# Sigmoid attention and a SiLU MLP on one core: a quad's heads regrouped so that one DMA loads all 128 partitions

## The chip, the cores and the metric

The kernel runs on one core of a Trainium2 chip. The metric is the device time of one execution in microseconds; before the change it is 379.75 us, the median of three runs (379.59 to 379.92).

The engines are named as in the profile. PE multiplies matrices, and PEld is its load of the stationary operand ("weights"); DVE and ACT work elementwise and move results out of PSUM; POOL here only makes an identity matrix and issues DMAs; SP issues DMAs. Transfers themselves run on 16 DMA engines that all queues share.

## The reference

Cut to what matters, in float32:

```python
q, k, v: (8, 12, 448, 64)          # batch, heads, sequence, head_dim
w_in: (768, 2048); w_out: (2048, 768)

scores = q @ k.T / sqrt(64) - log(448)
attn = sigmoid(scores) @ v                       # per batch and head
x = attn.transpose(0, 2, 1, 3).reshape(8 * 448, 12 * 64)
h = x @ w_in
out = (h * sigmoid(h)) @ w_out                   # (3584, 768)
```

A column of `x`, and so a row of `w_in`, belongs to one head and one of its 64 dimensions.

## The kernel before

**Quads and units.** Attention works in 24 quads: a batch and four of its 12 heads (`g = 3 * b + iq`). A quad's q, k or v lies in one tile `[128, 2, 7, 64]` in fp16 (`qf`, `kf`, `vf`; `new_flat`, line 66): the lower 64 partitions hold two heads (`j` = 0, 1), the upper 64 two others. A partition holds 7 neighbouring rows of the sequence, so the 448 rows are 64 partitions by 7 chunks. Before the change the lower half has heads `2 * iq` and `2 * iq + 1`, the upper half heads `6 + 2 * iq` and `7 + 2 * iq`; `load` (line 71) therefore issues two DMAs per tile, each over 64 partitions, from POOL, which converts float32 to fp16 on the way (112 KB written for each half).

A unit is one quad and one of its 7 chunks of keys (168 units). `scores` (line 177) makes 4 matmuls of a unit into PSUM (`psc`, two buffers), and ACT turns them into `attnT` with one sigmoid (line 202). `values` (line 213) multiplies them with `vf` in 7 rounds of 4 matmuls (`pav`), one round per unit, and DVE moves the two sums of a quad into `xT[b]`, whose 6 column blocks are pairs of heads. q and k must be transposed first: for quads 0 to 5 on PE through an identity matrix (`pe_transpose`, line 140), for the others by a DMA (`dma_transpose`, line 159) after DVE or ACT has put the rows in order.

**The MLP.** `h_unit` (line 250) makes one of 16 blocks of h per batch, 6 matmuls on `xT` and `w_in_sb`, with a sigmoid on ACT and a product on DVE. `out_set` multiplies with `w_out`. `w_in_sb` holds the 768 rows of `w_in` as 6 blocks of 128 partitions, one for each pair of heads; `load_w_in` (line 106) loads a quarter of the 2048 columns, which four h units use, with one DMA.

**What sets the order.** Every engine runs its instructions in the order in which the kernel writes them down. POOL's queue is: the first two chunks of k of quad 0, the identity, the rest of that k, then k and q of quad 1, v of 0, k and q of 2, v of 1 and 2, k and q of 3, and the first quarter of w_in (lines 455 to 464); later loads are written down behind transposes and values (`after_transpose`, `after_values`). POOL's DMAs take eight semaphores in turn, so that an issue waits for the landing of the eighth DMA before it. The first q does not go through POOL: SP and ACT load it as float32 into a spare tile (`load_first_q`, line 89), and DVE (chunks 0 to 3) and ACT (chunks 4 to 6) convert it (lines 469 and 470). Before it is there, PE runs nine dummy matmuls.

The first 24 units are followed by a table written by hand, `behind` (line 542), which says what PE does after the scores of each unit: dummy matmuls (`keep_busy`), transposes, some rounds of `values` (`rounds`), and, as the first work on w_in, four of the six matmuls of h units 0 and 1 (`begin`). After unit 23 the order comes from `stretch` (line 435), which deals out MLP matmuls between bursts of scores by a budget of nanoseconds.

Of the kernel before, what the change touches and what calls it, by code (L numbers as in the profile page):

```python
# [17 lines left out]
def kernel(  # L18
# [9 lines left out]
    nc = tc.nc  # L28

    B, H, S, D = q.shape  # L30
    NT, DMODEL = out.shape
    DFF = moe_w_in.shape[1]
    P = 128
    HP = P // 2
    NCH = S // HP
    NPAIR = H // 2
    NQ = NPAIR // 2
# [22 lines left out]

    source = {"q": q, "k": k, "v": v}
    flat = {}

    def new_flat(name, g):
        flat[name, g] = (p3 if name == "v" else p4).tile(
            [P, 2, NCH, D], F16, tag=f"{name}f", name=f"{name}f"
        )

    def load(names, g, c0=0, c1=NCH):
        b, iq = divmod(g, NQ)
        for name in names:
            if (name, g) not in flat:
                new_flat(name, g)
            for half in range(2):
                h0 = half * (H // 2) + 2 * iq
                nc.gpsimd.dma_start(  # L78
                    flat[name, g][half * HP : (half + 1) * HP, :, c0:c1].rearrange(
                        "p i c d -> p i (c d)"  # L80
                    ),
                    source[name][b, h0 : h0 + 2].rearrange("i (p c) d -> p i (c d)", c=NCH)[
                        :, :, c0 * D : c1 * D
                    ],
                )

    FIRST, SPLIT = 2, 4

    def load_first_q():
        room = cpool.tile([P, NHC * NO2 // 2], F32, tag="T2", name="qs")  # L90
        st = room[:, : 2 * NCH * D].rearrange("p (i c d) -> p i c d", i=2, c=NCH)
        for half, eng in ((0, nc.sync), (1, nc.scalar)):
            h0 = half * (H // 2)
            eng.dma_start(
                st[half * HP : (half + 1) * HP].rearrange("p i c d -> p i (c d)"),
                q[0, h0 : h0 + 2].rearrange("i (p c) d -> p i (c d)", c=NCH),
            )
        return st

    ident = cpool.tile([P, P], F16, tag="ident", name="ident")  # L100
    bias_s = cpool.tile([P, 1], F32, tag="biass", name="bias_s")
# [1 line left out]
    w_in_sb = cpool.tile([P, NCC, DFF], F16, tag="w_in_sb", name="w_in_sb")  # L103
    w_out_sb = cpool.tile([P, NFC, DMODEL], F16, tag="w_out_sb", name="w_out_sb")

    def load_w_in(step):
        cols = slice(step * DFF // 4, (step + 1) * DFF // 4)
        nc.gpsimd.dma_start(
            w_in_sb[:, :, cols], moe_w_in[:, cols].rearrange("(cc p) f -> p cc f", p=P)
        )  # L110

    def load_w_out(nh, part):
        cols = slice(nh * NO2, (nh + 1) * NO2)
# [23 lines left out]
    def act_copy(o, i):  # L137
        nc.scalar.activation(o, i, AF.Copy)
# [286 lines left out]
    def rows_if_any():  # L425
        if later:
            g, name = later.pop(0)
            dma_transpose(g, name, nc.vector.tensor_copy)
            if name == "q" and g + 4 < NQB and g + 4 > 12:
                load("kq", g + 4)  # L430
# [4 lines left out]
    def stretch(ns):  # L435
# [14 lines left out]
                middle = math.inf  # L450
        late_sigmoid()

    first_q = load_first_q()
    new_flat("q", 0)
    load("k", 0, 0, FIRST)
    make_identity(nc, ident)
    load("k", 0, FIRST, NCH)
    load("kq", 1)
    load("v", 0)
    load("kq", 2)  # L460
    load("v", 1)
    load("v", 2)
    load("kq", 3)
    load_w_in(0)

    nc.vector.memset(dummy, 0.5)
    nc.vector.memset(bias_s, NEG_LOG_S)
    nc.scalar.activation(warm, bias_s, AF.Sigmoid, bias=bias_s, scale=1.0)
    nc.vector.tensor_copy(flat["q", 0][:, :, :SPLIT], first_q[:, :, :SPLIT])
    act_copy(flat["q", 0][:, :, SPLIT:], first_q[:, :, SPLIT:])  # L470

    units = [(g, ch) for g in range(NQB) for ch in range(NCH)]
    waiting = []
# [3 lines left out]
    def after_transpose(g):  # L477
        if g == 0:
            load("kq", 4)
            load_w_in(1)  # L480
        elif g == 1:
            load("kq", 5)
        elif g == 4:
            load("kq", 8)

    def after_values(g):
        if g == 0:
            load("v", 3)
            load_w_in(2)
            load_w_in(3)  # L490
        elif g == 1:
            load("v", 4)
            load_w_out(0, 0)
            load_w_out(0, 1)
        elif g == 2:
            load("v", 5)
            load_w_out(1, 0)
            load_w_out(1, 1)
            load("kq", 6)
            load("kq", 7)  # L500
        elif g + 3 < NQB:
            load("v", g + 3)
        if g == 6:
            for to in (10, 11, 12):
                load("kq", to)
        if g == 5:
            load("kq", 9)
        if g >= 6 and g + 3 < NQB:
            later.extend(((g + 3, "k"), (g + 3, "q")))
# [28 lines left out]
    def begin(fc, steps):  # L538
# [20 lines left out]
        17: ((rounds, 1, 7),),  # L559
        18: ((rounds, 2, 2),),  # L560
        19: ((rounds, 2, 4),),
        20: ((begin, 0, 4),),
        21: ((rounds, 2, 6),),
        22: ((rounds, 2, 7),),
        23: ((begin, 1, 4),),
    }
# [68 lines left out]
```

## Time and profile before

| | us |
|---|---|
| median of the runs | 379.75 |
| the profiled execution | 379.66 |
| its span on the core | 377.9 |
| PE busy | 368.4 (97%) |
| ACT busy | 242.7 (64%) |
| DVE busy | 234.2 (62%) |
| POOL busy, mostly issuing DMAs | 93.2 (25%) |

The chain that ended last is PE for 90% of the span. Its other shares stand in the first 26 us: DMA 3%, POOL 4%, ACT 2%. By line, PE's share is 39% in `ph` (h, line 257), 34% in `po` (output, line 333), 9% in the scores (line 191) and 7% in the values (line 227).

The granted clock of PE is full throughout. The DMA engines are busy for 80% or more of nearly every slice in the first 90 us, at up to 205 GB/s written; that counts the fp16 bytes, and twice as many float32 bytes are read for them. A busy DMA share above 1 means that packets overlap on an engine.

How to read the rows: a group's row gives the line, the engine, the operation, output and inputs by the program's names, the number of instructions, their busy time in us and the mean of one in ns, then the idle time of the engine just before them and what ended it. A row of waits gives who waited for whom: total us, times, longest. A row of the chain or of a timeline begins with its start in us and its duration.

### The profile page before, as it was taken

To read this page: it belongs to the slowest core of one execution; us is meant where nothing else is said; L and a number is where in the kernel's file an instruction comes from. 1 tells how busy PE (TensorE), PEld (TensorE's weight loads), DVE (VectorE), ACT (ScalarE), POOL (GpSimd) and SP (SyncE) were. 2 spreads that over 40 slices of the span, in tenths; PEclk is the share of its full clock that TensorE was granted. 3 is DMA by queue.
4 is the path that set the end of the run, shared out by engine and by line. 5 is a ranking of instruction groups with operands and counts; after the bars stand their busy time and mean duration, and the time that the engine had idled before them with its cause. 6 is when DMAs were issued, how large, how long until landed. Compare 5 with 4: busy or idle time off the path is not lost.

```text
span 377.9 us, 7695 instructions
## 1 busy us (share of the span) xinstructions
PE 368.4 (97%) x3081; PEld 189.1 (50%) x3081; DVE 234.2 (62%) x417; ACT 242.7 (64%) x355; POOL 93.2 (25%) x158
## 2 busy tenths in 40 slices
PE   6989999999999999999999999999999999999995
PEld 2544445555554445545555544544555455555663
DVE  2546646996666566648577557645677457556773
ACT  4998886868777776576556676667866685244000
POOL 8846325402744304303132303101011000000000
PEclk9999999999999999999999999999999999999999
DMA  8999999994999999929399856745065300110233
GB/s 126 179 189 204 205 203 166 135 146 95 170 195 140 179 111 120 149 61 112 62 166 193 94 117 93 76 111 75 0 136 97 84 2 2 50 35 0 81 87 83
DMA packets 66403, 42.80 MB, mean 113 GB/s; under 512 B 37056, under 2 KB 62912, under 8 KB 66368
## 3 DMA queue, kind: packets, MB, share of 16 engines
q0 software_dynamic: 28032, 22.59, 44.3%
q1 hardware_dynamic: 38112, 19.41, 30.5%
q8 instruction: 24, 0.39, 0.4%
q10 hardware_dynamic: 224, 0.33, 0.3%
q14 instruction: 11, 0.09, 0.1%
HBM read 45.61 MB, written 11.01 MB: 150 GB/s over the span
## 4 chain that ended last, share of the span: by engine, by line
PE 90%; POOL 4%; DMA 3%; ACT 2%; issue 1%; DVE 0%; ACTq 0%; POOLq 0%
PE ph L257 39%; PE po L333 34%; PE psc L191 9%; PE pav L227 7%; DMA w_in_sb<-in_moe_w_in_dram 3%; POOL kf L78 2%; ACT attnT L202 1%; POOL vf L78 1%; POOL qf L78 1%; PE ptrq L148 0%; PE ptrk L148 0%; ACT attnT L175 0%; DVE gTr L271 0%; DVE osb L341 0%; ACT kept L402 0%
## 5 line engine op out<-in xcount | busy, mean ns | idle before, releaser
L202 ACT ACTIVATE attnT<-psc,bias_s 128x896 f16<-128x896 f32 (+1 forms) x168 | 138.1, 900 | 46.3 <-PE psc L191 46.3
L257 PE MATMUL ph<-xT,w_in_sb 128*128 128x448 f16 x768 | 151.1, 353 | 0.8 <-DMA w_in_sb<-in_moe_w_in_dram 0.8
L271 DVE TENSOR_TENSOR gTr<-ph,tsig 128x448 f16<-128x448 f32 x128 | 78.2, 622 | 69.3 <-ACT tsig L269 68.8
L257 PEld LDWEIGHTS <-w_in_sb 128*128 128x128 f16 x768 | 72.9, 98 | 74.2 <-issue 8.0
L269 ACT ACTIVATE tsig<-ph 128x448 f16<-128x448 f32 x128 | 68.2, 548 | 49.5 <-PE ph L257 49.2
L78 POOL DMA_DIRECT2D vf<-in_v_dram x48 | 28.9, 619 | 141.1 <-PE pav L227 119.8
L333 PEld LDWEIGHTS <-S 128*128 128x128 f16 x448 | 42.3, 98 | 33.5 <-issue 7.2
L341 DVE SCALAR_TENSOR_TENSOR osb<-po,osb 128x384 f32<-128x384 f32 x70 | 37.6, 553 | 22.8 <-PE po L333 22.4
L191 PE MATMUL psc<-qT,kT 64*64 64x448 f16 x672 | 48.4, 360 | 2.3 <-ACT attnT L202 0.9
L238 DVE TENSOR_SCALAR xT<-pav 128x448 f16<-128x448 f32 x48 | 27.7, 619 | 31.5 <-PE pav L227 31.5
L333 PE MATMUL po<-T,S 128*128 128x384 f16 x224 | 40.6, 327 | 0.0
L333 PEld LDWEIGHTS <-gTr 128*128 128x128 f16 x304 | 28.7, 98 | 23.5 <-issue 5.4
L333 PE MATMUL po<-w_out_sb,S 128*128 128x384 f16 x224 | 39.9, 326 | 0.0
L227 PE MATMUL pav<-attnT,vf 64*64 64x448 f16 x672 | 38.1, 349 | 0.4 <-DVE gTr L271 0.4
L78 POOL DMA_DIRECT2D qf<-in_q_dram x46 | 27.6, 612 | 31.5 <-DMA w_out_sb<-in_moe_w_out_dram 12.6
L333 PE MATMUL po<-w_out_sb,gTr 128*128 128x384 f16 x192 | 34.9, 327 | 0.0
L78 POOL DMA_DIRECT2D kf<-in_k_dram x50 | 30.3, 618 | 10.7 <-DMA vf<-in_v_dram 4.4
L191 PEld LDWEIGHTS <-kT 64*64 64x64 f16 x672 | 16.4, 105 | 30.3 <-issue 26.1
L175 ACT ACTIVATE attnT<-psc,bias_s 128x896 f16<-128x896 f32 x26 | 26.5, 1021 | 0.0
L341 DVE SCALAR_TENSOR_TENSOR osb<-po,m 128x384 f32<-128x384 f32 x42 | 23.2, 552 | 5.3 <-PE po L333 4.2
L227 PEld LDWEIGHTS <-vf 64*64 64x64 f16 x672 | 20.5, 107 | 12.0 <-issue 1.9
L348 ACT ACTIVATE m<-po 128x384 f32<-128x384 f32 x14 | 6.9, 494 | 23.7 <-PE po L333 23.7
(42 smaller groups left out, 152.2 us busy)
## 6 DMA issues: line engine op xcount, KB each, us to landing
out_dram<-osb SPq DMA_DIRECT2D x54, 192.0 KB, 3.0
vf<-in_v_dram POOLq DMA_DIRECT2D x48, 112.0 KB, 4.6
kf<-in_k_dram POOLq DMA_DIRECT2D x46, 112.0 KB, 5.9
qf<-in_q_dram POOLq DMA_DIRECT2D x46, 112.0 KB, 6.1
w_in_sb<-in_moe_w_in_dram POOLq DMA_DIRECT2D x4, 768.0 KB, 10.7
w_out_sb<-in_moe_w_out_dram POOLq DMA_DIRECT2D x4, 768.0 KB, 17.0
kT<-kr SPq DMA_TRANSPOSE x18, 5.9
qT<-qr SPq DMA_TRANSPOSE x18, 6.7
```

Source lines behind the costliest of these rows:

```text
L78: nc.gpsimd.dma_start(flat[name, g][half * HP : (half + 1) * HP, :, c0:c1].rearrange("p i c d -> p i (c d)"), source[name][b, h0 : h0 + 2] ...
L175: nc.scalar.activation(to, psc, AF.Sigmoid, bias=bias_s, scale=QKSCALE)
L191: nc.tensor.matmul(banks[j][own, :S], qkT["k", g][rows, ch, own], qkT["q", g][rows, :, own], start=True, stop=True,)
L202: nc.scalar.activation(to, psc, AF.Sigmoid, bias=bias_s, scale=QKSCALE)
L227: nc.tensor.matmul(pav[half][j * D : (j + 1) * D, :S], flat["v", g][own, j, ch, :], at[own, j, :], start=(ch == 0), stop=(ch == NCH - 1),)
L238: nc.vector.tensor_scalar_mul(xT[b][:, half * NQ + iq, :], pav[half][:, :S], SX)
L257: nc.tensor.matmul(ph[:, :S], w_in_sb[:, cc, fc * P : (fc + 1) * P], xT[b][:, cc, :], start=(at == 0), stop=(at == NCC - 1),)
L269: nc.scalar.activation(tsig, ph[:, :S], AF.Sigmoid, bias=0.0, scale=ISX)
L271: nc.vector.tensor_mul(gTr[:, fc, (b % 2) * S : (b % 2) * S + S], ph[:, :S], tsig)
L333: nc.tensor.matmul(po[:, :NO2], a[:, fc, :], w[:, fc, :], start=(fc == 0), stop=(fc == NHC - 1))
L341: nc.vector.scalar_tensor_tensor(out=o, in0=po, scalar=sign, in1=x, op0=ALU.mult, op1=ALU.add)
L348: nc.scalar.activation(m1, po, AF.Copy, scale=ISX)
```

## The change

The grouping of heads changes. A quad is now four neighbouring heads `4 * iq` to `4 * iq + 3`, with head `4 * iq + 2 * j + h` in slot `j` of half `h`. Two neighbouring heads then fill 128 partitions at one even step through memory, so one DMA loads a whole tile (`rows_in`). Each pair of heads in `xT` is now heads that are two apart, and `w_in`'s rows must be permuted to match: a block of 128 partitions takes 64 rows of one head and 64 of another that is not its neighbour. `load_w_in` does this with four DMAs of 64 partitions and three blocks each. The first q is cut between SP and ACT by chunks and no longer by halves of the partitions, so each of the two casts reads what one DMA brought. In the table, two entries change places: rounds 4 and 5 of values(2) now stand after unit 20, and the first four matmuls on w_in after unit 21.

The number of instructions on PE, DVE and ACT stays the same; on POOL the rows of the program go from 159 to 103.

```diff
+    def rows_in(name, g):
+        b, iq = divmod(g, NQ)
+        return source[name][b, 4 * iq : 4 * iq + 4].rearrange(
+            "(i h) (p c) d -> (h p) i (c d)", h=2, c=NCH
+        )
+
     def load(names, g, c0=0, c1=NCH):
-        b, iq = divmod(g, NQ)
         for name in names:
             if (name, g) not in flat:
                 new_flat(name, g)
-            for half in range(2):
-                h0 = half * (H // 2) + 2 * iq
-                nc.gpsimd.dma_start(
-                    flat[name, g][half * HP : (half + 1) * HP, :, c0:c1].rearrange(
-                        "p i c d -> p i (c d)"
-                    ),
-                    source[name][b, h0 : h0 + 2].rearrange("i (p c) d -> p i (c d)", c=NCH)[
-                        :, :, c0 * D : c1 * D
-                    ],
-                )
+            nc.gpsimd.dma_start(
+                flat[name, g][:, :, c0:c1].rearrange("p i c d -> p i (c d)"),
+                rows_in(name, g)[:, :, c0 * D : c1 * D],
+            )
...
-        st = room[:, : 2 * NCH * D].rearrange("p (i c d) -> p i c d", i=2, c=NCH)
-        for half, eng in ((0, nc.sync), (1, nc.scalar)):
-            h0 = half * (H // 2)
+        at = 0
+        for c0, c1, eng in ((0, SPLIT, nc.sync), (SPLIT, NCH, nc.scalar)):
+            size = 2 * (c1 - c0) * D
+            st = room[:, at : at + size]
+            at += size
             eng.dma_start(
-                st[half * HP : (half + 1) * HP].rearrange("p i c d -> p i (c d)"),
-                q[0, h0 : h0 + 2].rearrange("i (p c) d -> p i (c d)", c=NCH),
+                st.rearrange("p (i e) -> p i e", i=2), rows_in("q", 0)[:, :, c0 * D : c1 * D]
             )
-        return st
+            yield flat["q", 0][:, :, c0:c1], st.rearrange("p (i c d) -> p i c d", i=2, d=D)
...
     def load_w_in(step):
         cols = slice(step * DFF // 4, (step + 1) * DFF // 4)
-        nc.gpsimd.dma_start(
-            w_in_sb[:, :, cols], moe_w_in[:, cols].rearrange("(cc p) f -> p cc f", p=P)
-        )
+        rows = moe_w_in[:, cols].rearrange("(iq j h d) f -> h j d iq f", j=2, h=2, d=D)
+        for half in range(2):
+            for j in range(2):
+                nc.gpsimd.dma_start(
+                    w_in_sb[j * D : (j + 1) * D, half * NQ : (half + 1) * NQ, cols], rows[half, j]
+                )
...
-    first_q = load_first_q()
     new_flat("q", 0)
+    casts = list(load_first_q())
...
-    nc.vector.tensor_copy(flat["q", 0][:, :, :SPLIT], first_q[:, :, :SPLIT])
-    act_copy(flat["q", 0][:, :, SPLIT:], first_q[:, :, SPLIT:])
+    nc.vector.tensor_copy(*casts[0])
+    act_copy(*casts[1])
...
-        20: ((begin, 0, 4),),
-        21: ((rounds, 2, 6),),
+        20: ((rounds, 2, 6),),
+        21: ((begin, 0, 4),),
```

## The prediction

> **What bounds the kernel now.** I read the page first, then the waits of PE, then the chain that ended last between 15 and 33 us, then ACT's timeline, and last the landing of each early DMA.
>
> ```profile
> span 377.9 us, 7695 instructions
> PE 368.4 (97%) x3081; PEld 189.1 (50%) x3081; DVE 234.2 (62%) x417; ACT 242.7 (64%) x355; POOL 93.2 (25%) x158
> L257 PE MATMUL ph<-xT,w_in_sb 128*128 128x448 f16 x768 | 151.1, 353 | 0.8 <-DMA w_in_sb<-in_moe_w_in_dram 0.8
> L78 POOL DMA_DIRECT2D qf<-in_q_dram x46 | 27.6, 612 | 31.5 <-DMA w_out_sb<-in_moe_w_out_dram 12.6
> ```
>
> PE is busy for 97% of the span; POOL, whose work the change halves, for 25%. So the change can only pay where PE is idle, or where it is busy but held to another engine's pace. The waits of PE are few:
>
> ```profile
> PE pw L135 <- DVE bias_s L467: 1.5, 1, 1.5
> PE psc L191 <- ACT attnT L202: 0.9, 2, 0.5
> PE ph L257 <- DMA w_in_sb<-in_moe_w_in_dram: 0.8, 1, 0.8
> PE psc L191 <- ACT qT L138: 0.6, 1, 0.6
> PE pav L227 <- DVE gTr L271: 0.4, 1, 0.4
> PE ptrq L148 <- DVE qf L469: 0.3, 1, 0.3
> ```
>
> Two of them touch the change: the wait for w_in (0.82 us) and that for the first q (0.32 us). The chain and ACT's timeline put the first in its place:
>
> ```profile
> 15.13 10.77 DMA w_in_sb<-in_moe_w_in_dram
> 25.90 0.05 issue
> 25.95 0.93 PE ph L257 x4
> ...
> 27.30 1.02 ACT attnT L202
> 28.32 0.04 issue
> 28.36 0.38 PE psc L191 x4
> 28.74 2.57 PE ph L257 x13
> ```
> ```profile
> 5.26 0.52 ACT L138 ACTIVATE qf<-qs 128x384 f16<-128x384 f32 x1 [2.17 <-DMA qs<-in_q_dram]
> 7.53 18.96 ACT L202 ACTIVATE attnT<-psc,bias_s 128x896 f16<-128x896 f32 x21 [0.56 <-PE psc L191]
> 27.30 2.80 ACT L202 ACTIVATE attnT<-psc,bias_s 128x896 f16<-128x896 f32 x3 [0.82 <-PE psc L191]
> ```
>
> From 7.53 to 26.49 us ACT runs 21 sigmoids without a gap (18.96 / 21 = 0.90 us each); PE follows ACT. Then PE stands for the first quarter of w_in (25.12 to 25.95), ACT starves for 0.82 us, and only from 28.7 us is PE the bound. From there to 373.69 us PE is busy for all but 0.5 us (344.47 of 344.99). So **the run's length is the time at which the score unit 23 starts on PE (28.36 us) plus a fixed amount of work**, unless a later transfer comes late.
>
> The landings: from about 6 to 66 us POOL's loads land strictly one behind another; in the clean part each 112 KB tile half comes 0.56 us after the one before and each 768 KB quarter of w_in takes 3.8 us. Both are 205 GB/s, as the window 30 to 35 us shows (204 GB/s, DMA share 1.25). That stream is bound by its bytes, not by the number of its DMAs. The first w_in quarter took 6.36 us (last q half of quad 3 landed at 19.54, w_in at 25.90): the windows from 18 to 24 us have 162, 172 and 184 GB/s.
>
> **The change, part by part.**
>
> *One DMA for two halves.* A quad's q, k or v cost POOL two issues of 0.62 us; now one, of twice the packets. The w_in quarter, six times the packets of a half tile, took 0.87 us, so linear between these rows one takes about 0.67 us. Ahead of w_in 22 issues become 11. This frees POOL, which is no bound, and moves no byte: within the saturated stream it is worth nothing. It can help where the stream is not yet full: from 4 to 6 us the windows show 136 and 129 GB/s, and the second part of the first k is issued only at 3.10. With one issue instead of two ahead of it, that moves about 0.6 us up. I take 0.4 us for the whole stream (bounds 0, if POOL's issue is no limit there, and 0.7).
>
> *First q by chunks.* Before, each queue carries one half of the partitions and both casts wait for the later (ACT's landed at 4.20, SP's at 5.18). Now SP carries chunks 0 to 3 for DVE's cast, ACT chunks 4 to 6 for its own. The packet records show that the two queues are served in turn: SP's first packet starts (2.94) when ACT's eight on that DMA engine are through. ACT's 1792 B packets took 74 ns, SP's mostly 110 to 150. By 1536 B (65 ns) and 1792 B (74 ns) rows a 1024 B packet is 47 ns and a 768 B one 38 ns: per DMA engine 16 x 38 + 16 x 47 = 1.36 us against 8 x 74 + 8 x 130 = 1.63. If SP's packets were slow because all wrote the lower 64 partitions, that goes, and q is whole about 0.4 us sooner; but the dummy matmuls (1.46 + 4.02) hold PE to 5.48, so no more than 0.32 us of it counts. If they were slow for another reason, SP's share is 16 x 47 x 130/74 = 1.32 us, the sum 1.93, and q comes 0.3 us later; if the denser k stream, which now runs beside it, also takes a turn for each packet, up to 0.5. I take -0.15 (bounds -0.32 and +0.5), nearer to the even spread, since both transfers now cover all partitions. The first k chunk, one issue instead of two (the second landed at 5.63), should be there by about 5.4; PE wants it at 5.99. All that follows moves with this: the sigmoids are back to back.
>
> *The swap in the table.* After unit 20 now stand rounds 4 and 5 of values(2), after unit 21 the four matmuls on w_in. Take the old pace of ACT: unit 20's scores at 24.74 to 25.12; round 4 needs unit 18's sigmoid (done), round 5 unit 19's (done about 25.7, 1.02 us from 24.68), for which unit 21's scores wait as well. So the rounds end near 25.84, unit 21's scores near 26.2, ahead of ACT's turn for it at 26.49. w_in is wanted at 26.03, 0.9 us later than before. The four matmuls end at 26.79, unit 22's scores at 27.17, ahead of ACT's turn at 27.39, and unit 23's can start when sigmoid 21 ends, at 27.50. That is 28.36 - 27.50 = 0.86 us gained, if w_in is there by 26.0. It landed at 25.90 before; less the stream's 0.4 us and with the need 0.15 earlier, 0.5 us are to spare. If that cover is gone, each us that w_in lands later than 26.1 costs nearly one.
>
> *w_in in four pieces.* Twelve more issues of about 0.63 us on POOL, 7.6 us in all, behind nobody who waits: eight POOL DMAs may be in flight, and the loads queued behind (quad 4's k and q, v of 3) were landed 4.7 and 1.8 us before PE used them. Bytes and packet sizes are the same. The weights' first wait on PE is now on two landings, twice; nothing is queued that could run. Half-height transfers of 112 KB ran at the same 205 GB/s as the full-height w_in, so I take a piece at 0.96 us and the extra at 0. The other bound: if lower-half pieces suffer as SP's q packets did (130/74), a quarter takes 3.84 + 2 x 0.96 x 0.76 = 5.3 us. The second quarter (landed 32.05, wanted at 33.7, now 32.7) has then -1.9 us to spare.
>
> By the Trainium skill, "DMA: Bandwidth & Descriptors", section "Rules for kernel authors", two transfers to disjoint partition halves do not run beside each other and one 128-partition transfer is better; that speaks for the first part and against this one. With the fit in its section on one DMA's anatomy (2.0 us and bytes / 436e3, an estimate) a quarter in four pieces would take 11.6 us against 5.6, and the sum would turn to several us slower. The 0.56 us between landings in this trace disagree with a fixed 2 us for DMAs that are queued.
>
> *Further on.* Transposed k and q were landed at least 1.0 us before PE's use (quad 6), the loads of v after 60 us 20 us before; a shift of 1 us leaves that as it is, since what they wait for shifts too. The tail is untouched.
>
> **Sum.** Profiled execution 379.66 us (span 377.9 and 1.8 around it): -0.86 - 0.15 = -1.01, so 378.65. The median of the runs, 379.75, lies 0.09 above it: **378.7**. A measurement of this kernel tells about 0.2% (0.76 us) from no change.
>
> **Rivals.**
>
> A, the forecast: stall gone, q 0.15 us sooner (0.3 either way). 378.7, from 378.2 to 379.0. For it: ACT's unbroken row, and w_in's need that moves 0.9 us. Chance 0.55. If 0.4 us of the later waits (DVE gTr, 49.27 us) also falls away, 378.0.
>
> B, the first q becomes the new wait: twice the packets per queue, SP's served last and slow, k's stream beside it. The stall is gone, the sigmoids start 0.3 to 0.5 us later: 379.75 - 0.86 + 0.4 = 379.3. For it: SP's 110 to 150 ns. Against: ACT's 74. This holds the case that merged DMAs do nothing at all, since the stream is bound by bytes: with q unmoved it gives 378.9. Chance 0.27.
>
> C, slower: the half-height pieces of w_in, lower halves slow. It decides once a quarter takes 1 us more than before. Quarter 1 then lands at 25.9 - 0.4 + 1.46 = 27.0 against a need at 25.9, 0.2 of it covered: +0.9; quarter 2 at 34.6 against 32.7 + 0.9: +1.0; quarter 3 (39.2, wanted at 42.7) has room. 379.75 - 1.01 + 1.9 = 380.7. Against: the even 0.56 us of lower and upper halves. Chance 0.18.
>
> So faster 0.55, same 0.27, slower 0.18; the range runs from A's lower end, 378.0, to C, 380.7.
>
> **What would show it.** Right: no wait of PE for w_in; ACT's sigmoids 0 to 23 in one row; unit 23's scores near 27.4; DVE's first cast at 5.1 or before. B shows as a cast after 5.3 and first sigmoid after 7.53. C shows as w_in pieces landing more than 1.2 us apart and PE waiting for them at about 26 and 33 us. A PE wait after 60 us would be none of these, and would make the prediction wrong.

## The result and the profile after

After the change the kernel takes 382.69 us (median of 22 runs, 379.70 to 384.77) against 379.67 before on the same chips (22 runs, 378.77 to 380.66): ratio 1.0068, 95% interval 1.0047 to 1.0089. The kernel became slower, against a forecast of 378.7 (378.0 to 380.7). The median stands for two kinds of run: 14 of the 22 have a mean granted clock of 0.996 or less and take 382.15 to 384.77 us, the other 8 have 0.998 or more and take 379.70 to 381.26. The profiled execution took 383.01 us, 3.35 more than that of before.

From the page of the kernel after, the span and the rows that answer to those of before:

```profile
span 381.2 us, 7622 instructions
...
PE 370.3 (97%) x3081; PEld 189.4 (50%) x3081; DVE 234.2 (61%) x417; ACT 243.2 (64%) x355; POOL 65.8 (17%) x98
...
L261 PE MATMUL ph<-xT,w_in_sb 128*128 128x448 f16 x768 | 151.2, 353 | 0.0
...
L195 PE MATMUL psc<-qT,kT 64*64 64x448 f16 x672 | 48.8, 361 | 4.4 <-DMA qT<-qr 2.6
```

POOL has lost 27 us of work, and the idle time ahead of `ph`, the wait for w_in, is 0.0. But the scores now have 2.6 us of idle time that a DMA ended, and PE is busy for 1.9 us more with the same 3081 matmuls. The scores' row before had no DMA in it:

```profile
L191 PE MATMUL psc<-qT,kT 64*64 64x448 f16 x672 | 48.4, 360 | 2.3 <-ACT attnT L202 0.9
```

ACT's timeline shows the start as forecast, with the 24 sigmoids in one row:

```profile
4.10 0.52 ACT L142 ACTIVATE qf<-qs 128x384 f16<-128x384 f32 x1 [1.24 <-DMA qs<-in_q_dram]
...
7.06 21.89 ACT L206 ACTIVATE attnT<-psc,bias_s 128x896 f16<-128x896 f32 x24 [0.55 <-PE psc L195]
```

The waits of PE name what is new, and the chain that ended last gives its place (start, duration, what):

```profile
PE psc L195 <- DMA qT<-qr: 2.6, 1, 2.6
PE pw L139 <- DVE bias_s L471: 1.5, 1, 1.5
PE psc L195 <- ACT qT L142: 0.6, 1, 0.6
```
```profile
93.39 0.36 PE po L337 x2
93.74 13.56 DMA qT<-qr
107.31 0.14 issue
107.44 0.49 PE psc L195 x4
```

A transposing DMA of q, issued on SP at 93.74 us, is done 13.56 us later; scores of quad 9 wait for it. The windows (start and end, length, then busy time and instructions of PE, PEld, DVE, ACT and POOL, then the granted clock, DMA share and GB/s) show PE at rest from 105 to 107 us, and afterwards busy, but at half the clock:

```profile
105.00:107.00 2.00, 0.00 (x0) 0.00 (x0) 1.14 (x2) 1.83 (x3) 0.00 (x0) 1.00 1.26 194
107.00:109.00 2.00, 1.56 (x8) 0.71 (x9) 0.00 (x0) 0.97 (x1) 0.00 (x0) 0.65 1.23 192
109.00:111.00 2.00, 2.00 (x7) 0.88 (x6) 1.16 (x2) 0.04 (x1) 0.00 (x0) 0.50 1.25 194
```

Before, PE is busy there at full clock:

```profile
105.00:107.00 2.00, 2.00 (x21) 0.88 (x20) 1.14 (x2) 1.76 (x5) 2.00 (x4) 1.00 1.26 239
107.00:109.00 2.00, 2.00 (x17) 1.09 (x18) 1.71 (x3) 1.77 (x2) 0.65 (x2) 1.00 1.40 163
```

**Where the time went.** The start of each score unit on PE against the same unit before (us, minus is earlier) puts a place to every gain and loss. Some units, with the kernels of the experiments that the text below uses:

```
unit  before    after  e1     e2     e3     e4     e5     e6
   0    7.09   -0.47  -0.88  -0.96  -0.04  +0.01  -0.76  -0.55
  23   28.36   -1.38  -1.27  -1.17  -0.95  -0.58  -1.41  -1.37
  42   79.32   -1.26  -1.16  -0.59  -0.83  -0.43  -1.29  -1.26
  48   86.44   -1.26  -1.15  -0.32  -0.83  -0.43  -1.29  -0.56
  59  101.78   -1.26  -1.15  +0.80  -0.83  +0.01  -1.29  -0.56
  62  105.54   -1.11  -1.15  +0.80  -0.83  +0.00  -1.29  -0.56
  63  105.73   +1.71  -0.25  +0.80  +2.19  +0.01  -1.29  -0.56
  64  108.89   +3.37  -0.23  +0.80  +2.21  +0.01  -1.29  -0.56
 167  320.16   +3.37  -0.22  +0.80  +2.21  +0.01  -1.29  +0.02
span  377.85   +3.39  -0.24  +0.77  +2.27  -0.00  -1.31  -0.00
```

After: 1.26 us of lead up to unit 59, 0.15 lost at unit 61 (just after DVE has waited 1.6 us for the load of quad 10's q; the link is not isolated), 2.82 at unit 63, the first of quad 9, another 1.66 at 64, nothing from there on: -1.26 + 0.15 + 2.82 + 1.66 = 3.37. The forecast gain was there, and one place near 105 us took it back more than threefold.

**Why the transpose is late.** POOL's timeline shows what is issued just ahead of it, after and before:

```profile
90.98 0.71 POOL L82 DMA_DIRECT2D vf<-in_v_dram  x1 [28.32 <-PE pav L231]
...
97.11 0.76 POOL L82 DMA_DIRECT2D qf<-in_q_dram  x1
98.63 0.72 POOL L82 DMA_DIRECT2D vf<-in_v_dram  x1 [0.76 <-PE pav L231]
```
```profile
100.46 0.59 POOL L78 DMA_DIRECT2D kf<-in_k_dram  x1 [0.78 <-DMA kf<-in_k_dram]
...
102.24 0.59 POOL L78 DMA_DIRECT2D qf<-in_q_dram  x1 [0.55 <-DMA qf<-in_q_dram]
...
105.24 1.23 POOL L78 DMA_DIRECT2D vf<-in_v_dram  x2
```

`after_values(6)` writes down the loads of quads 10, 11 and 12 at one place (lines 507 to 509). After, they and quad 13's go out from 91.0 to 97.9 us, nine whole tiles; the last lands at 110.8. Before, the same bytes were spread by POOL's eight places: each held 112 KB, and rows such as the one at 100.46 wait for a landing. An equal number of places now holds twice the bytes. The packet records show what that does to a transpose. In after from 102 to 106 us the two queues get nearly the same number of packets: 172 to 178 per us of the transposes (256 B, 31 ns each) and 164 to 167 of the loads (896 B, 87 ns). With few loads beside it or none, a transpose runs at 880 packets per us (quad 10's k before, from 105 to 106 us) to 1021 (quad 9 in e5, from 95 to 96 us). So beside loads that never let up, the transposes ran about five times slower here.

The Trainium skill, "DMA: Bandwidth & Descriptors", section "Queues, rings and completion order", says that a DMA engine goes round the queues that have work, packet by packet. The nearly equal counts, such as 178 against 166 from 105 to 106 us, agree with it; the records do not tell which engine a packet ran on.

### The profile page after: what moved, and what is told of

Same layout as the page of the kernel before. It is cut to its first block, busy times and chain, and to the rows that moved or that the text cites. A ratio compares the mean times of both kernels' runs of the same rounds, so it can differ in the third digit from the quotient of the medians.

```text
span 381.2 us, 7622 instructions
## 1 busy us (share of the span) xinstructions
PE 370.3 (97%) x3081; PEld 189.4 (50%) x3081; DVE 234.2 (61%) x417; ACT 243.2 (64%) x355; POOL 65.8 (17%) x98
## 4 chain that ended last, share of the span: by engine, by line
PE 88%; ACT 6%; DMA 4%; issue 1%; DVE 0%; ACTq 0%
PE ph L261 38%; PE po L337 32%; PE psc L195 9%; PE pav L231 7%; ACT attnT L206 5%; DMA qT<-qr 4%; PE pw L139 1%; PE ptrq L152 0%; PE ptrk L152 0%; ACT attnT L179 0%; DVE gTr L275 0%; DVE osb L345 0%; ACT kept L406 0%; ACT m L352 0%; DVE dummy L470 0%
## 5 line engine op out<-in xcount | busy, mean ns | idle before, releaser
L82 POOL DMA_DIRECT2D vf<-in_v_dram x24 | 17.2, 720 | 181.2 <-PE pav L231 156.9
L337 PE MATMUL po<-T,S 128*128 128x384 f16 x224 | 41.4, 331 | 0.0
L337 PEld LDWEIGHTS <-gTr 128*128 128x128 f16 x304 | 28.8, 98 | 23.9 <-issue 6.0
L337 PE MATMUL po<-w_out_sb,gTr 128*128 128x384 f16 x192 | 35.8, 331 | 0.0
L179 ACT ACTIVATE attnT<-psc,bias_s 128x896 f16<-128x896 f32 x26 | 26.5, 1021 | 1.2 <-PE psc L195 1.2
L82 POOL DMA_DIRECT2D kf<-in_k_dram x25 | 18.2, 727 | 18.8 <-DVE kr L167 8.6
L337 PE MATMUL po<-T,gTr 128*128 128x384 f16 x112 | 21.4, 326 | 0.0
```

Of the source, the lines that this page charges most:

```text
L82: nc.gpsimd.dma_start(flat[name, g][:, :, c0:c1].rearrange("p i c d -> p i (c d)"), rows_in(name, g)[:, :, c0 * D : c1 * D],)
L179: nc.scalar.activation(to, psc, AF.Sigmoid, bias=bias_s, scale=QKSCALE)
L337: nc.tensor.matmul(po[:, :NO2], a[:, fc, :], w[:, fc, :], start=(fc == 0), stop=(fc == NHC - 1))
```

## The experiments

The theory after the result: (1) the doubled bytes in flight starve the DMA transposes of quad 9; (2) the wait that follows costs its length, and after it the halved clock; (3) the start of the run keeps its gain. The rivals were that w_in's pieces, the swap or the first q carry the loss, and that the loads' number and not their place in time matters. Each kernel was compared with the kernel before on the same chip. The lead table above is of the profiled executions.

**e1_defer**: after, with the loads of quads 10 to 12 written down one quad each; quad 13's stay where they were.

```diff
-        if g == 6:
-            for to in (10, 11, 12):
-                load("kq", to)
+        if g in (6, 7, 8):
+            load("kq", g + 4)
```

> The changed kernel with one edit: the loads of k and q for quads 11 and 12 are no longer issued together with those of quad 10 but one quad later each (behind values 7 and 8). Theory 1 (backlog): in the changed kernel POOL's eight DMAs in flight are 224 KB each and not 112, so the loads of quads 10 to 12 lie all at once beside the DMA transposes of quad 9 and take every second packet; qT of quad 9 lands at 107.3 us and PE waits 2.6 us, then runs at a granted clock of 0.5 to 0.65 for some 4 us. With fewer loads beside it qT of quad 9 lands before 104 us, no wait of PE for qT, clock 1.0 throughout, time 378.4 (1.3 us under the kernel before, since unit 23 started 1.4 us sooner). Theory 2 (layout): the regrouped, whole-height loads or their strides are slow in themselves, and the number in flight does not matter: a wait for a transpose of 2 us or more stays, time 381.5 or more.

Measured: 379.34 us, ratio 1.0004 (0.9978 to 1.003; single runs from 378.04 to 382.65). PE's wait for qT falls from 2.6 to 0.7 us, qT lands at 105.34 instead of 107.31, and the clock stays full behind it. Less beside the transposes, less late: theory 1, in part. I had expected qT before 104 us and no wait, but five tiles are still issued from 91.1 to 95.1 us and five more from 98.7 us on, before qT has landed.

**e2_halves**: after, with every load of k, q and v in two halves again.

```diff
+            for half in range(2):
+                own = slice(half * HP, (half + 1) * HP)
+                nc.gpsimd.dma_start(
+                    flat[name, g][own, :, c0:c1].rearrange("p i c d -> p i (c d)"),
+                    rows_in(name, g)[own, :, c0 * D : c1 * D],
+                )
```

> The changed kernel with each k, q and v tile loaded by two DMAs of 64 partitions again, in the new grouping of heads; w_in in four pieces, first q by chunks and the table stay as changed. Theory 1 (backlog): eight DMAs in flight are 112 KB each again, the queue runs dry between loads as before, qT of quad 9 lands near 102 us, no wait for it, time 378.4 to 378.8. Theory 2 (layout): the new grouping stays, so the wait stays, 381.5 or more.

Measured: 380.36 us, ratio 1.0027 (1.0008 to 1.0046). qT of quad 9 lands at 101.66 and PE doesn't wait for it, as theory 1 has it. But the lead of 1.17 us is lost on the way, in steps, to +0.80 at unit 59; neither theory nor rival had this. The second of these waits of PE is the place of the last step, 1.12 us (the first lies in the first 40 us):

```profile
PE ptrq L154 <- DMA qf<-in_q_dram: 1.4, 3, 0.9
PE psc L197 <- DVE osb L347: 1.0, 1, 1.0
```

DVE stands behind its copy of quad 10's k: half of that tile lands at 101.35 and the copy starts at 101.43. Before, the same landing was at 100.18 and the copy started at 100.64, the next one 0.08 us after q's landing. So the kernel before already runs there at the pace of its loads, and whoever arrives earlier waits. I had not seen this margin.

**e3_cover**: after, with 13 dummy matmuls ahead of the scores that wait, so that PE is busy during the wait.

```diff
+            if u == (9, 0):
+                keep_busy(13)
```

> The changed kernel with 13 dummy matmuls (2.8 us at full clock) on PE ahead of the first scores of quad 9, so that PE works where it waited for qT. Splits the loss into wait and clock. If the fall of the clock follows from the idle time (theory 1a): the clock stays at 1.0, the wait is covered but not gone, and the 1.6 us that the low clock cost are saved: 381.0 to 381.4. If the clock falls for another reason (theory 1b): clock again 0.5 to 0.65 near 108 us and 382.7 or more.

Measured: 381.83 us, ratio 1.0054 (1.0035 to 1.0074). qT is as late as before this edit (107.06), and the loss at unit 63 is 3.02 us, but at 64 it is 0.02 instead of 1.66. The time gains less than I had expected (381.0 to 381.4), for the dummy matmuls are too many: they follow each other until 107.8 us, though qT is there at 107.06, so part of the 3.02 us is theirs. Its windows, the first two of those shown for after:

```profile
105.00:107.00 2.00, 2.00 (x14) 0.93 (x11) 0.50 (x1) 2.00 (x3) 0.00 (x0) 1.00 1.27 195
107.00:109.00 2.00, 2.00 (x14) 0.88 (x13) 0.00 (x0) 0.63 (x2) 0.00 (x0) 1.00 1.23 192
```

The granted clock stays at 1.00. The 1.66 us of after are therefore the clock's, and its 2.82 at unit 63 the wait's.

**e4_swap**: the kernel before, with nothing but the two table entries exchanged.

```diff
-        20: ((begin, 0, 4),),
-        21: ((rounds, 2, 6),),
+        20: ((rounds, 2, 6),),
+        21: ((begin, 0, 4),),
```

> The kernel before with the two table entries swapped and nothing else. The prediction's step: w_in is wanted 0.9 us later, the wait of 0.82 us for it goes, ACT's row of sigmoids has no gap, unit 23 starts 0.86 us sooner, time 378.8. Rival: w_in's first quarter then lands later or another wait takes its place, time 379.5 or more.

Measured: 379.31 us, ratio 0.9994 (0.998 to 1.0009). The lead is 0.58 us at unit 23, less than the 0.86 of the sum, because w_in's first quarter lands at 26.47 us here (25.90 before) and PE still waits 0.29 us for it. At unit 59 the lead is gone: DVE's two copies for quad 10 wait for their loads again (landed 100.56 and 102.39, copies at 100.64 and 102.47).

**e5_spread**: after, with the loads of k and q four quads ahead, one quad at a time.

```diff
-            if name == "q" and g + 4 < NQB and g + 4 > 12:
-                load("kq", g + 4)
...
-        if g == 6:
-            for to in (10, 11, 12):
-                load("kq", to)
         if g == 5:
             load("kq", 9)
+            load("kq", 10)
+        elif 6 < g < NQB - 4:
+            load("kq", g + 4)
```

> The changed kernel with the loads of k and q from quad 10 on spread out: quad 10 directly behind quad 9 (free once ACT has copied quad 6, about 64 us), the later ones one quad per values, instead of quads 10 to 13 at 91 to 97 us. Only v of quad 9 then stands beside the DMA transposes of quad 9. Theory (the gain of the start is given back near 100 us to DMA transposes and copies that wait for their share of the DMA engines): neither PE waits for qT of quad 9 nor DVE for k and q of quad 10, the lead of 1.2 to 1.4 us at unit 23 is kept to the end, 378.1 to 378.4 against 379.4 for the kernel before. Rival (the lead is lost to something that the number of loads does not touch): a loss of 0.5 us or more between units 57 and 66 again, 379.0 or more.

Measured: 378.76 us, ratio 0.9962 (0.9945 to 0.9979): faster than both kernels, though I had expected 378.1 to 378.4. The lead of 1.29 us is kept to the end. The issues of DMAs from 92 to 94.5 us with the time to landing, first after, then e5:

```profile
kT<-kr SPq DMA_TRANSPOSE x1, 9.7
qT<-qr SPq DMA_TRANSPOSE x1, 13.6
```
```profile
kT<-kr SPq DMA_TRANSPOSE x1, 3.5
qT<-qr SPq DMA_TRANSPOSE x1, 3.0
```

The last load beside them, v of quad 9, has landed at 94.95 us; the transpose of q takes 3.0 us from issue to landing instead of 13.6. Nothing else of the change was undone: theories 1 and 3 hold.

**e6_halves_spread**: e5 with the half loads of e2.

> As e5_spread, but with each k, q and v tile loaded by two DMAs of 64 partitions. Theory: merging two half loads into one is worth nothing by itself, only the number of bytes in flight differs; with the loads spread both are alike, 378.1 to 378.6, and the lead at unit 23 is kept. Rival: whole-height loads are faster or slower in themselves by 0.5 us or more.

Measured: 380.34 us, ratio 1.0013 (0.9997 to 1.0029). I had taken whole-height loads for worth nothing in themselves; that is a miss, since they are all that parts e6 from e5, 1.6 us in the medians. e6 loses its lead in steps up to the end (-1.37, -0.56, +0.02). The windows from 60 to 70 us of e5 and then of e6:

```profile
60.00:65.00 5.00, 5.00 (x28) 2.60 (x27) 2.91 (x7) 3.82 (x7) 2.19 (x4) 1.00 1.26 202
65.00:70.00 5.00, 5.00 (x29) 2.56 (x27) 4.68 (x10) 4.37 (x8) 0.47 (x1) 1.00 1.27 196
```
```profile
60.00:65.00 5.00, 5.00 (x28) 2.62 (x27) 2.88 (x6) 3.09 (x5) 2.33 (x4) 1.00 1.20 183
65.00:70.00 5.00, 5.00 (x28) 2.56 (x27) 4.09 (x9) 5.00 (x10) 4.77 (x9) 1.00 1.28 154
```

With half loads the stream runs at 183 and 154 GB/s, with whole ones at 202 and 196; before, which loads quad 10 only later, had 150 and 134. ACT of e6 then waits 0.5 and 0.8 us for k and q that it copies. That these waits make the first loss is argued from the rows, not isolated.

**e7_swap_spread** and **e8_before_spread**: the edit of e5 on e4 and on the kernel before.

> The kernel before with the swap in the table and the loads spread as in e5_spread, old grouping, old first q, w_in in one DMA. The swap alone led by 0.44 us until unit 57 and had nothing left at unit 59. Theory: with the loads spread the 0.44 us (up to 0.6) stay, 378.8 to 379.0. Rival: nothing left again, 379.3 or more.

> The kernel before with the loads spread as in e5_spread and nothing else. PE has no wait between 50 and 268 us in the profile of before, so theory and rival both expect no change from it, 379.3 to 379.5; a gain here would mean that the spread is worth something of its own and that its gain in e5_spread is not the lead kept.

Measured: e7 380.21 us, ratio 1.0009 (0.9985 to 1.0033); e8 379.98 us, 1.0006 (0.9988 to 1.0025). e7's runs scatter from 378.8 to 383.36 and its profiled start is late by itself (+0.59 at unit 0, and a granted clock of 0.50 from 8.8 to 15.6 us), so it decides nothing. e8 shows that spreading brings the old kernel nothing: what e5 gains is the change's, once its place is free.

**e9_spread_again, e10, e11, e12**: e5 once more, and e5 with one part of the change undone: the old table order (e10), the first q by halves of the partitions, with both casts waiting for both (e11), w_in's quarter in one DMA (e12, whose h units therefore multiply the wrong heads).

```diff
+        20: ((begin, 0, 4),),                                   # e10
+        21: ((rounds, 2, 6),),
...
+        for half, eng in ((0, nc.sync), (1, nc.scalar)):        # e11
+            own = slice(half * HP, (half + 1) * HP)
+                st[own].rearrange("p i c d -> p i (c d)"), rows_in("q", 0)[own]
...
+            w_in_sb[:, :, cols], moe_w_in[:, cols].rearrange("(cc p) f -> p cc f", p=P)   # e12
```

> The kernel of e5_spread once more, as the partner of the three that follow on the same chip. 0.5 to 1.2 us faster than the kernel before, as in e5_spread.

> e9 with the table entries 20 and 21 in the old order. In the changed kernel the first quarter of w_in has landed at 22.8 us, 3 us before it is wanted even in the new order. Theory: the swap is worth nothing beside the earlier w_in, time within 0.2 us of e9. My prediction's account (the swap brings 0.86 us): 0.5 to 0.9 us slower than e9.

> e9 with the first q loaded by halves of the partitions again (new heads), so that both casts wait for both queues. Theory: the loads by chunks brought the first sigmoid from 7.53 to 7.06 us, so 0.4 to 0.5 us slower than e9, first sigmoid at 7.5. Rival: the later loads set the pace by unit 20 anyway, less than 0.2 us.

> e9 with each quarter of w_in loaded by one DMA over 128 partitions again, its rows in the old order, so that the products on w_in mix the wrong heads. Theory 1 (pieces cost nothing): the first quarter lands near 23 us as in e9 and the time is within 0.2 us of e9; the slow first quarter of the kernel before (6.4 us) was then not due to its being one DMA. Theory 2 (one big DMA starves the queue of its eight places): it lands after 25 us, PE waits for it, 0.5 us or more slower than e9.

Measured against the same runs of before (379.33 us):

```
                       us     ratio  interval           unit 23   span
e9_spread_again        378.32 0.9969 0.9955 to 0.9982   -1.18    -1.05
e10_spread_old_table   378.59 0.9971 0.9957 to 0.9984   -1.17    -1.16
e11_spread_q_halves    379.02 0.9983 0.9967 to 0.9999   -0.66    -0.56
e12_spread_w_in_one    378.59 0.9970 0.9955 to 0.9985   -1.61    -1.44
```

The gain of e5 repeats. The swap is worth nothing beside the rest that these runs can tell (e10). w_in in four pieces costs nothing that these runs can tell (e12). The first q by chunks is worth 0.7 us in the medians and 0.5 in the profiles (e11), although the two intervals overlap. DVE's first cast in e9 and in e11:

```profile
3.92 0.43 DVE L471 CAST qf<-qs 128x512 f16<-128x512 f32 x1 [2.51 <-DMA qs<-in_q_dram]
```
```profile
5.58 0.43 DVE L470 CAST qf<-qs 128x512 f16<-128x512 f32 x1 [4.17 <-DMA qs<-in_q_dram]
```

## Why the prediction was wrong

For the first 30 us the sum came near, in part for other reasons than it gave; two steps on what follows failed.

- **Failed: "moves no byte: within the saturated stream it is worth nothing".** The bytes are the same, but eight places in flight hold twice as many of them. The transposes go through another queue, which got about as many packets as the loads did (178 and 166 per us), so the backlog of the loads decided when the transposes were done. qT of quad 9 came at 107.31 us instead of 101.74, and PE had all else ready at about 104.6. Price: 2.82 us of wait, 1.66 of clock (e3). Undone by timing alone in e5, by size alone in e2.
- **Failed: "Further on … a shift of 1 us leaves that as it is, since what they wait for shifts too".** I looked at the smallest margin of the landings before (1.0 us at quad 6) and let everything shift with it. The transposes do not wait only for their source: their rate depends on what POOL has in flight, and quad 9 is where twelve tiles are put down close together (v9, v10 and k and q of 10 to 14). Nor does the margin at quad 10, 0.08 us between landing and copy, let an earlier PE keep its lead (e2, e4). The text named the sign that would refute it: a PE wait after 60 us.
- **The swap, -0.86: right in size, but not needed beside the whole-height loads.** In e2, where w_in's first quarter lands at 26.00 us, the lead grows by 0.86 us from unit 20 to unit 23. Alone the swap gives 0.58 us at unit 23, as the quarter comes too late (e4), 0.43 from unit 42 and nothing from unit 59. In after the quarter is there early, at 22.81 us and not 25.5, and then the stall is gone without the swap too (e10: landed at 21.70, and from unit 20 to 23 the lead grows by 0.89 us all the same).
- **The stream, "0.4 us for the whole stream (bounds 0 ... and 0.7)": mis-sized, it was 3.1 us.** In the kernels with half loads that quarter landed between 23.9 and 26.5. The premise that POOL "is no bound" did not hold at the start: before, POOL issues from 3.10 to 16.0 us with hardly a pause, and the quarter goes out at 15.13 us; after, at 10.66. The windows from 8 to 12 us show 135 and 167 GB/s before, 171 and 186 after. POOL's issues alone do not explain it, since 112 KB per issue of 0.59 us would be 194 GB/s; what else makes half loads slower is open.
- **First q by chunks, -0.15 (bounds -0.32 and +0.5): right sign, too small.** -0.47 in the profile, -0.5 to -0.7 by e11. SP's part landed at 3.86 instead of 5.18 us. The bound of 0.32 fell too, since the first transposes started at 5.33, not 5.48. One profile says little of this size: unit 0 lies between -0.96 and -0.04 in the nine kernels with the new q (mean -0.54), between -0.35 and +0.59 in the five with q by halves (mean +0.10). With the new q, which is there by 4.4 us, the dummy matmuls are the last thing PE has to finish. They start 0.43 us apart at first and 0.22 once the clock has risen (the page's row of the clock shows it as full from the start), and unit 0 comes in the order in which the traces record that rise, from 4.20 us (e2, -0.96) to 7.03 (e3, -0.04).
- **w_in in four pieces, 0.96 us each, extra 0: right.** The first four landed at 19.90, 20.89, 21.85 and 22.81. Rival C fell with that (e12), and so did rival B: the cast was early.
- **POOL's issue of a whole tile, 0.67 us:** 0.72 measured, of no consequence.

That unit 23 came near the forecast, -1.38 us against -1.01, is thus partly luck: the stall did go, but two causes removed it, each enough alone (e2, e10), and what the first q brought hangs on when the clock rises. That the runs of after scatter over 5 us (379.70 to 384.77), those of e5 over 0.9, fits a wait that ends sooner or later and, where it is long, takes the clock down with it; only one run of each was traced.

## What to carry to other kernels

Where a kernel limits its DMAs in flight by number, as the eight semaphores of POOL do here, doubling their size doubles the bytes in flight, and a transfer of another queue can come later for it, as qT did; go through the transfers of the other queues at the place where most loads are issued at once, not where the margin was smallest before. Then put the loads down at the pace at which they are used: the same change went from 1.0068 (1.0047 to 1.0089) to 0.9962 (0.9945 to 0.9979) when k and q were loaded one quad at a time. And a lead won at the start is only worth what the tightest landing further on lets through, so list those margins before adding up a gain.

## What the runs showed of the hardware

- 2.57 us without a matmul was enough for the granted clock to fall to 0.50, from 107.6 to 111.0 us, which cost 1.66 us on top. The Trainium skill, "TensorE: Matmul & The Clock Gate", section "What's actually happening", gives about 3.4 us of idle time for that; here it was less. Thirteen dummy matmuls during the wait kept the clock (e3).
- A DMA transpose that took 3.0 us from issue to landing (e5) took 13.6 beside the loads of nine tiles (after), at nearly equal packet counts for both queues (178 and 166 per us).
- Two DMAs of the first q, on SP and ACT, landed at 3.76 to 4.05 us and 3.99 to 4.36 over all partitions (nine kernels), at 4.77 to 5.58 and 4.20 to 4.94 by halves (five kernels), for the same bytes.
